# Pooled attention and a top-1 mixture of experts on one core: the first two pairs of heads are turned on TensorE instead of VectorE

## The chip, the core and the metric

The kernel runs on one core of a Trainium2 chip. The metric is the device time of one execution in microseconds (us), as the median of several runs. A difference of less than about 0.2% between two versions can't be told from none.

## What is computed

The reference, cut to what matters. Batch 8, 8 heads, 1152 positions, head dimension 64; then 4608 tokens of 512 go to one of 8 experts each.

```python
def _attn_ref(q, k, v):
    q_pool = q.reshape(B, H, S // 2, 2, D).mean(axis=3)      # two neighbouring queries become one
    scores = 1.0 / np.sqrt(D) * np.matmul(q_pool, k.transpose(0, 1, 3, 2))
    scores = scores - np.max(scores, axis=-1, keepdims=True)
    attn = np.exp(scores)
    attn = attn / (np.sum(attn, axis=-1, keepdims=True) + 1e-09)
    return np.matmul(attn, v)

def _moe_ref(x, w_gate, w1, w2):
    logits = x @ w_gate
    expert_idx = np.argmax(logits, axis=1)
    gate_w = softmax(logits)[np.arange(N), expert_idx]
    for e in range(E):
        mask = expert_idx == e
        out[mask] = gate_w[mask, None] * (np.maximum(x[mask] @ w1[e], 0.0) @ w2[e])
```

## The kernel before, in words

Attention goes by pairs of heads: 8 batches of 4 pairs, 32 pairs in all. For a pair, keys, queries and values are loaded (`load_pair`, L474), keys and queries are brought into a layout with the head dimension on the partitions (`kT`, `qT`: two heads of 64 on the 128 partitions), and then each half of the 576 pooled queries (288 columns) goes through these steps:

- **scores** (L556): 9 blocks of keys. A block is four products of 64x64 weights with 288 moving columns in the four quarters of the array (L573). VectorE copies each block from PSUM into `s`, scaled, and keeps the least value (L577, "eviction"). After the ninth block the stabilizer is reduced and spread (L598, L595, L601: `top`, `bias`).
- **exponentials**: ScalarE, two blocks at a time, in place (L605).
- **row sums** (`chunk_sum`, L635): GpSimd adds the nine blocks into three, in two additions of 128x1728 and a third of 128x576 (L661, L665, "folds"), and TensorE adds the rest (L655, L648).
- **values** (L696): 9 blocks of four products (L709) into `pa`, then `xT`.

How keys and queries are turned before: the loads put 32 numbers of a head's row beside each other on a partition, so every run in memory is 128 bytes long (`quarters`, L488). VectorE then transposes in squares of 32 (`turn_k`, L535: three instructions of 128x384 for a pair; `turn_q`, L540: two of 128x288). Before that the two neighbouring queries are added, for the first pair on VectorE (L516), for the others on GpSimd (L527). The first pair (`opening`, L484) has its keys loaded in two parts, and the queries of the first two pairs are asked for by ScalarE's queue (L501). All other loads come from SyncE (SP), in the order of its stream.

What sets the order: every step is recorded in a `Flow` (L96) with an engine, a cost in ns and a key. `emit` (L126) plays the steps through with these costs and writes each engine's instructions in the order in which they would start. The chip then runs each engine's stream in order, with semaphores between them. So costs that are given to a step shape the order, not the time. Buffers have numbers of places: three pairs of PSUM banks `st` for scores (also used by row sums and the spread), four of `s`, two of `kp`, one each of `qn` (raw queries) and `qp` (added queries). With one place for `qn`, a load of queries waits until the ones before are used up.

TensorE begins with two products of ones with 512 columns (`warm_up`, L1358), before any data is there.

After attention come the experts; their order on TensorE is the same before and after the change.

## Time and profile before

| | us |
|---|---|
| median of three runs | 1130.89 (1130.54 to 1132.59) |
| the profiled execution | 1137.59 |
| its span | 1135.8 |
| attention, until the last values | about 672 |

The profile has the busy time of each engine, a timeline of instructions in order of time, the chain of work that ended last, and busy times by stretch. In a timeline row stand the start, the duration (of a merged run of instructions: from the first start to the last end), the engine, the line and operation, the tiles, and in brackets the idle time before with what ended it. A product in 32-bit floats stands there as two records, so a block of four products is "x8". Rows on "SPq" or "ACTq" are DMA issues. A record of TensorE includes some 0.2 us after the columns have streamed, so records overlap, and a busy TensorE need not be at its peak.

### The profile page before, as it was taken

Reading aid. Unit: us, or ns where it says so; the run is one execution under the profiler, and the core shown is the slowest. Engines: PE = TensorE matmul, PEld = TensorE weight load, DVE = VectorE, ACT = ScalarE, POOL = GpSimd, SP = SyncE. Lnnn points to the kernel's source line nnn. Section 1 sums busy time; section 2 is a strip of 40 time slices with the busy share of each in tenths; the row PEclk is TensorE's granted clock in tenths of the full one; section 3 lists DMA queues with packets and bytes.
Section 4 is the critical chain, followed back from the end, with each engine's and each line's share of the span. In section 5 each row is a group of like instructions: output and inputs, shape, how many; then the busy total and the mean of one; then the engine's idle time right before and its main releaser. Section 6 shows DMA issues by size and latency. Waiting matters only on the chain.

```text
span 1135.8 us, 32903 instructions
## 1 busy us (share of the span) xinstructions
PE 1109.3 (98%) x13233; PEld 790.7 (70%) x13233; DVE 879.8 (77%) x2250; ACT 617.2 (54%) x831; POOL 851.2 (75%) x488
## 2 busy tenths in 40 slices
PE   7999999999999999999999998999999999999997
PEld 3556565565565565565655557988899989899986
DVE  6988988988988988989989849866556655567761
ACT  1666565565656556656557346444444544465551
POOL 1999999999999999999999852577566655445421
PEclk9999999999999999999999999999999999999999
DMA  9976756737747648647544417855556656667740
GB/s 133 153 135 102 150 80 115 122 51 133 120 65 129 105 71 136 99 79 137 97 80 95 134 50 219 229 173 165 168 179 200 196 171 187 197 224 261 244 157 30
DMA packets 398111, 158.07 MB, mean 139 GB/s; under 512 B 314454, under 2 KB 368626, under 8 KB 397950
## 3 DMA queue, kind: packets, MB, share of 16 engines
q1 hardware_dynamic: 378014, 133.93, 54.9%
q0 software_dynamic: 10464, 20.78, 5.9%
q10 hardware_dynamic: 9472, 1.18, 0.9%
q8 instruction: 106, 1.74, 0.7%
q14 instruction: 55, 0.45, 0.2%
HBM read 135.02 MB, written 22.07 MB: 138 GB/s over the span
## 4 chain that ended last, share of the span: by engine, by line
PE 69%; DVE 17%; issue 7%; DMA 3%; POOL 2%; ACT 1%; SPq 0%; POOLq 0%; ACTq 0%; DVEq 0%
PE pa L709 17%; PE st L573 16%; PE py L1321 16%; PE ph L1291 14%; DVE s L577 9%; DVE kT L537 2%; PE st L655 2%; DVE row L876 2%; PE st L648 1%; POOL fold L665 1%; DMA kp<-in_k_dram 1%; DMA qn<-in_q_dram 1%; DVE lw L799 1%; DVE st L812 0%; ACT w2h L1248 0%
## 5 line engine op out<-in xcount | busy, mean ns | idle before, releaser
L605 ACT ACTIVATE s<-s,bias 128x1152 f32<-128x1152 f32 (+1 forms) x320 | 351.2, 1152 | 185.2 <-DVE bias L601 183.5
L577 DVE TENSOR_SCALAR_CACHE_REDUCE s<-st 128x576 f32<-128x576 f32 x576 | 417.2, 749 | 42.9 <-PE st L573 30.6
L573 PE MATMUL st<-qT,kT 64*64 64x288 f32 x4608 | 364.0, 410 | 11.2 <-DVE s L577 4.4
L709 PE MATMUL pa<-s,vn 64*64 64x288 f32 x4608 | 351.6, 404 | 1.1 <-DVE xT L716 0.7
L573 PEld LDWEIGHTS st<-qT,kT 64*64 64x64 f32 x4608 | 167.3, 134 | 134.2 <-DVE s L577 41.6
L709 PEld LDWEIGHTS pa<-s,vn 64*64 64x64 f32 x4608 | 174.8, 133 | 106.0 <-DVE xT L716 11.4
L665 POOL TENSOR_TENSOR fold<-s 128x1728 f32<-128x1728 f32 x55 | 212.9, 3872 | 19.9 <-ACT s L605 19.2
L665 POOL TENSOR_TENSOR fold<-fold,s 128x1728 f32<-128x1728 f32 x55 | 212.8, 3869 | 0.9
L1291 PE MATMUL ph<-xh,w1h 128*128 128x248 f32 (+4 forms) x512 | 154.3, 301 | 2.3 <-DVE hl L1301 2.2
L1291 PE MATMUL ph<-xl,w1h 128*128 128x248 f32 (+4 forms) x512 | 153.3, 299 | 0.2 <-DVE xl L1165 0.2
L1291 PE MATMUL ph<-xh,w1l 128*128 128x248 f32 (+4 forms) x512 | 152.9, 299 | 0.0
L1165 DVE TENSOR_TENSOR w2l<-raw,w2h 128x1024 fp32r<-128x1024 f32 x64 | 78.1, 1222 | 80.0 <-ACT w2h L1248 72.3
L1022 POOL DMA_INDIRECT xr<-x_runs,ix x76 | 91.4, 1202 | 50.8 <-issue 24.5
L1321 PE MATMUL py<-w2h,hh 128*128 128x512 f32 x328 | 128.1, 391 | 0.0
L1321 PE MATMUL py<-w2l,hh 128*128 128x512 f32 x328 | 127.8, 390 | 0.0
L1321 PE MATMUL py<-w2h,hl 128*128 128x512 f32 x328 | 127.8, 390 | 0.0
L1330 POOL DMA_INDIRECT out_dram<-y,rec x41 | 44.4, 1082 | 86.5 <-ACT y L1338 67.2
L1299 ACT ACTIVATE hh<-ph 128x372 fp32r<-128x372 f32 (+4 forms) x100 | 49.3, 493 | 110.0 <-PE ph L1291 102.1
L1291 PEld LDWEIGHTS ph<-xh,w1h 128*128 128x128 f32 x512 | 96.1, 188 | 5.2 <-DVE hl L1301 3.9
L1291 PEld LDWEIGHTS ph<-xl,w1h 128*128 128x128 f32 x512 | 96.2, 188 | 1.2 <-DVE xl L1165 0.4
L1291 PEld LDWEIGHTS ph<-xh,w1l 128*128 128x128 f32 x512 | 96.1, 188 | 0.0
L1022 POOL DMA_INDIRECT xq<-x_runs,ix x52 | 61.5, 1182 | 45.1 <-PE py L1321 22.1
(219 smaller groups left out, 1326.1 us busy)
## 6 DMA issues: line engine op xcount, KB each, us to landing
raw<-in_moe_w_dram SPq DMA_DIRECT2D x128, 512.0 KB
kp<-in_k_dram SPq DMA_DIRECT2D x124, 144.0 KB
vn<-in_v_dram SPq DMA_DIRECT2D x124, 144.0 KB
qn<-in_q_dram SPq DMA_DIRECT2D x120, 144.0 KB
x_runs<-row SPq DMA_DIRECT2D x96, 99.0 KB
xr<-x_runs,ix POOLq DMA_INDIRECT x76
x_runs<-empty SPq DMA_DIRECT2D x4, 297.0 KB
qn<-in_q_dram ACTq DMA_DIRECT2D x16, 72.0 KB
```

The source lines that it names most:

```text
L537: nc.vector.transpose(view(kT.t.rearrange(f"p (c b i) -> p {order} i", b=NQD, i=BL)), view(kp.t.rearrange(f"p ({order}) d -> p {order} d", ...
L573: nc.tensor.matmul(pt.t[to, h, :HQ], x.kT.t[up, c * P + i * D:c * P + (i + 1) * D], x.qT.t[up, cols], start=True, stop=True, tile_position ...
L577: nc.vector.tensor_scalar(s.t[:, c], pt.t[:, :, :HQ], -SCALE, None, op0=ALU.mult, op1=ALU.min, accum_out=mx.t[:, c:c + 1],)
L605: nc.scalar.activation(s.t[:, c0:c0 + n], s.t[:, c0:c0 + n], AF.Exp, bias=bias.t, scale=-1.0)
L665: add = lambda to, a, b: nc.gpsimd.tensor_tensor(to, a, b, ALU.add)
L709: mark.made = nc.tensor.matmul(pa.t[cs, i, :HQ], x.vn.t[up, h, c, :], s.t[up, c, h], start=c == 0, stop=c == NC - 1, tile_position=(up.sta ...
L1022: ins = nc.gpsimd.indirect_dma_start(out=x.xr[i // NQD].t[:, i % NQD, :], out_offset=None, in_=xg, in_offset=bass.IndirectOffsetOnAxis(ap= ...
L1165: (nc.gpsimd if eng == "POOL" else nc.vector).tensor_tensor(lo, raw, hi.bitcast(F32), ALU.subtract)
L1291: mark.made = nc.tensor.matmul(view()[:, i, :], a[:, c, fp], b[:, c, :n], start=c == 0 and k == 0, stop=c == NDC - 1 and k == 2)
L1299: a = f.add("ACT", act(nb * n) - 44, lambda home=home, apart=apart: nc.scalar.activation(home(0), apart(), AF.Relu), at - 20, done(p), [ph ...
L1321: mark.made = nc.tensor.matmul(py.t, blocks(a)[:, c * x.nr + r], b[:, c % 2, :], start=c == 0 and k == 0, stop=c == NFC - 1 and k == 2)
L1330: ins = nc.gpsimd.indirect_dma_start(out=out, out_offset=bass.IndirectOffsetOnAxis(ap=x.re.t.bitcast(I32)[:, r, 0:1], axis=0), in_=y.t, in ...
```

## The change

For the first two pairs a new function, `first_pair`, takes the place of the loads, additions and transposes. Rows of the inputs are loaded as they lie in memory: a partition gets whole rows, 768 to 2304 bytes in a run for the keys and 4608 for the queries. TensorE multiplies them with the identity as the moving operand, which turns them: for the keys four products of 64x64 weights and 64 moving columns for a block (`cross_k`), for a half of the queries 36 products of 32 rows, 64 columns of weights and 32 moving columns (`cross_q`); the two neighbouring queries are added by accumulation in PSUM. Each result lands in a place of `st`; ScalarE copies one head's 64 partitions out, VectorE the other's. Values are loaded in one DMA for a pair. GpSimd and VectorE lose their additions and transposes for these two pairs.

```diff
-        opening = not o.exact and b == 0 and hp == 0
+        opening = not o.exact and b == 0 and hp < 2
...
+        if opening:
+            return first_pair(o, f, key, hp, x, kp, qn)
...
+    def first_pair(o, f, key, hp, x, kp, qn):
...
+        def load_k(c0, n):
+            for h, up in enumerate(both):
+                o.load(runs()[up, :, c0:c0 + n], heads(k, 0, hp)[h].rearrange("(i p c) d -> p i c d", i=2, c=NC)[:, :, c0:c0 + n])
+
+        def load_q(u, load):
+            for h in range(2):
+                load(pairs_()[h * D + u * BL:h * D + (u + 1) * BL].rearrange("p n d -> p (n d)"),
+                     heads(q, 0, hp)[h].rearrange("(i u n) d -> u i (n d)", i=BL, u=2)[u])
+
+        at = key + K_LOAD
+        cuts = [(0, NC)] if hp else [(0, FIRST), (FIRST, NC - FIRST)]
+        k0 = [f.carry("SP", 950, lambda c0=c0, n=n: load_k(c0, n), at + i, (), [kp], 100 + 300 * n, 1500 * i) for i, (c0, n) in enumerate(cuts)]
+        q0 = [f.carry("SP" if u or hp else "ACT", 950, lambda u=u: load_q(u, o.load if u or hp else side), at + 2 * u, (), [qn], 1400, 0 if hp else 2500 * u) for u in range(2)]
+        x.v = f.carry("SP", 500, lambda: o.load(vn.t.rearrange("p h c d -> p h (c d)"),
+                                                heads(v, 0, hp).rearrange("h (p c) d -> p h (c d)", p=P)), at + 3, (), [vn], 2700)
...
+        def turned(fn, ns, n, to, key, after, holds):
+            pt = score_banks(o)
+            t = f.add("PE", ns, lambda: fn(pt), key, after, [pt, *holds], QUADS)
+            copy = [(lambda up=up, h=h, eng=eng: eng(to.t[up, n], pt.t[up, h, :n.stop - n.start]))
+                    for h, (up, eng) in enumerate(zip(both, (nc.scalar.copy, nc.vector.tensor_copy)))]
+            made = done(*(f.add(e, w(n.stop - n.start), c, key, done(t), [pt, to]) for e, w, c in zip(("ACT", "DVE"), (act, dve), copy)))
...
+        def cross_k(c0, n, pt):
+            for c in range(n):
+                for i in range(2):
+                    for h, up in enumerate(both):
+                        at = (2 * c + i) * D
+                        nc.tensor.matmul(pt.t[up, h, at:at + D], runs()[up, i, c0 + c], ident[up, up], start=True, stop=True,
+                                         tile_position=(up.start, up.start))
+
+        def cross_q(u, pt):
+            for m in range(HQ // BL):
+                for t in range(2):
+                    for h, to in enumerate(both):
+                        up = slice(to.start + u * BL, to.start + (u + 1) * BL)
+                        nc.tensor.matmul(pt.t[to, h, m * BL:(m + 1) * BL], pairs_()[up, 2 * m + t], ident[up, up], start=t == 0, stop=t == 1,
+                                         tile_position=(up.start, to.start))
+
+        def turn_k(c0, n, at, got):
+            made = turned(lambda pt: cross_k(c0, n, pt), 220 * n, slice(c0 * P, (c0 + n) * P), kT, key + at, done(got), [kp])
...
+        def turn_q(u, at, got):
+            x.q[u] = turned(lambda pt: cross_q(u, pt), 1000, slice(u * HQ, (u + 1) * HQ), qT, key + at, done(got), [qn])
+
+        turn_k(0, FIRST, 0, k0[0])
+        turn_q(0, 1, q0[0])
+        for c0 in range(FIRST, NC, TURN):
+            turn_k(c0, min(TURN, NC - c0), 2 + c0 / 2, k0[-1])
+        turn_q(1, 7, q0[1])
```

Where instructions stand now. Lines after the change are 43 higher for scores, values and folds (L573 is L616, L709 is L752, L665 is L708); L574 are the products that turn keys, L582 those that turn queries.

TensorE at the start of the program, before; `st` are places in PSUM, and 16 blocks of scores follow each other:

```order
L1360 MATMUL st_210<-ones 128x512 x2
L573 MATMUL st_251<-qT_242,kT_249 64x288 x4
L573 MATMUL st_256<-qT_242,kT_249 64x288 x4
L573 MATMUL st_264<-qT_242,kT_249 64x288 x4
L573 MATMUL st_282<-qT_242,kT_249 64x288 x4
```

and after:

```order
L1403 MATMUL st_210<-ones 128x512 x2
L574 MATMUL st_230<-ident,kp_216 64x64 x12
L582 MATMUL st_243<-ident,qn_213 64x32 x36
L616 MATMUL st_286<-qT_283,kT_280 64x288 x4
L574 MATMUL st_291<-ident,kp_216 64x64 x12
L574 MATMUL st_307<-ident,kp_216 64x64 x12
L616 MATMUL st_322<-qT_283,kT_280 64x288 x4
L616 MATMUL st_329<-qT_283,kT_280 64x288 x4
L582 MATMUL st_335<-ident,qn_213 64x32 x36
L616 MATMUL st_373<-qT_283,kT_280 64x288 x4
```

Five turns (three of keys, two of queries) now stand in TensorE's stream, among the first three blocks of scores.

TensorE from the spread of the first stabilizer on, before (`pa` are the first values):

```order
L595 MATMUL st_375<-ident,top 64x64 x4
L573 MATMUL st_384<-qT_242,kT_249 64x288 x4
L573 MATMUL st_392<-qT_242,kT_249 64x288 x4
L709 MATMUL pa_403<-s_261,vn_231 64x288 x4
L573 MATMUL st_409<-qT_397,kT_389 64x288 x4
L709 MATMUL pa_403<-s_261,vn_231 64x288 x8
```

and after:

```order
L638 MATMUL st_448<-ident,top 64x64 x4
L616 MATMUL st_455<-qT_283,kT_280 64x288 x4
L574 MATMUL st_462<-ident,kp_225 64x64 x12
L582 MATMUL st_476<-ident,qn_380 64x32 x36
L616 MATMUL st_517<-qT_283,kT_280 64x288 x4
L616 MATMUL st_524<-qT_283,kT_280 64x288 x4
L752 MATMUL pa_530<-s_304,vn_223 64x288 x8
L574 MATMUL st_542<-ident,kp_225 64x64 x12
L574 MATMUL st_555<-ident,kp_225 64x64 x12
L616 MATMUL st_572<-qT_283,kT_280 64x288 x4
L752 MATMUL pa_530<-s_304,vn_223 64x288 x8
L582 MATMUL st_589<-ident,qn_380 64x32 x36
```

The spread stands after 13 blocks instead of 16, and all five turns of the second pair stand between the first values.

SyncE's loads, before (`kp` keys, `vn` values, `qn` queries; each `x4` with 32x36 is one pair):

```order
L485 DMA kp_218<-in_k_dram 32x12x32 x4
L485 DMA kp_218<-in_k_dram 32x24x32 x4
L485 DMA vn_231<-in_v_dram 32x9x64 x8
L485 DMA kp_244<-in_k_dram 32x36x32 x4
L485 DMA vn_298<-in_v_dram 32x2x576 x4
L485 DMA kp_314<-in_k_dram 32x36x32 x4
L485 DMA qn_414<-in_q_dram 32x36x32 x4
L485 DMA vn_443<-in_v_dram 32x2x576 x4
L485 DMA kp_474<-in_k_dram 32x36x32 x4
L485 DMA qn_572<-in_q_dram 32x36x32 x4
```

and after:

```order
L485 DMA kp_216<-in_k_dram 64x2x192 x2
L485 DMA kp_216<-in_k_dram 64x2x384 x2
L485 DMA qn_213<-in_q_dram 32x1152 x2
L485 DMA vn_223<-in_v_dram 128x2x576
L485 DMA kp_225<-in_k_dram 64x2x576 x2
L485 DMA vn_228<-in_v_dram 128x2x576
L485 DMA qn_380<-in_q_dram 32x1152 x4
L485 DMA kp_403<-in_k_dram 32x36x32 x4
L485 DMA qn_634<-in_q_dram 32x36x32 x4
L485 DMA vn_665<-in_v_dram 32x2x576 x4
L485 DMA kp_700<-in_k_dram 32x36x32 x4
L485 DMA qn_748<-in_q_dram 32x36x32 x4
```

14 issues for the first two pairs instead of 24 (and on ScalarE's queue 2 instead of 16). The queries of the third pair, `qn_414` before and `qn_634` after, have to wait for the place of the second pair's: before, until GpSimd had added them, now, until TensorE has done the last of the products on `qn_380`.

GpSimd's own stream, in words (a fold here is one addition of 128x1728): before, it held two folds, the addition of queries for the third pair, a third addition (128x576), two folds, a fold of the next pair, a third addition, a fold, the addition of queries for the fourth pair and a third addition. Now it holds two folds, a third addition, the addition of queries for the third pair, two folds, the addition of queries for the fourth pair, a third addition, two folds, an addition of queries and a third addition.

## Rows read from the trace of the kernel before

**Rows 1.** Busy time by stretch: start:end, us, then each engine with its instructions

```profile
core 0: us, PE busy (x) PEld busy (x) DVE busy (x) ACT busy (x) POOL busy (x), PEclk, DMA share, GB/s
28.00:100.00 72.00, 71.39 (x1171) 42.47 (x1160) 64.21 (x187) 47.60 (x51) 70.47 (x26) 1.00 0.74 130
```

**Rows 2.** Timeline of GpSimd, from the first fold on

```profile
28.23 3.87 POOL L665 TENSOR_TENSOR fold<-s 128x1728 f32<-128x1728 f32 x1 [6.04 <-ACT s L605]
...
37.21 1.41 POOL L527 TENSOR_TENSOR qp<-qn 128x576 f32<-128x576 f32 x1 [1.14 <-DMA qn<-in_q_dram]
...
39.93 3.88 POOL L665 TENSOR_TENSOR fold<-s 128x1728 f32<-128x1728 f32 x1
...
47.73 3.88 POOL L665 TENSOR_TENSOR fold<-s 128x1728 f32<-128x1728 f32 x1
...
59.52 7.71 POOL L665 TENSOR_TENSOR fold<-s 128x1728 f32<-128x1728 f32 x2
...
175.81 1.40 POOL L527 TENSOR_TENSOR qp<-qn 128x576 f32<-128x576 f32 x1 [2.56 <-DVE top L598]
```

**Rows 3.** Timeline of the opening: warm-up, first addition of queries, first scores, first exponentials

```profile
1.27 3.78 PE L1360 MATMUL st<-ones 128*128 128x512 f32 x4 [1.27 <-DVE ones L323]
...
7.47 0.46 DVE L516 TENSOR_TENSOR qp<-qn 128x288 f32<-128x288 f32 x1 [2.87 <-DMA qn<-in_q_dram]
...
8.96 3.16 PE L573 MATMUL st<-qT,kT 64*64 64x288 f32 x24 [3.90 <-DVE kT L537]
...
24.61 5.36 ACT L605 ACTIVATE s<-s,bias 128x1152 f32<-128x1152 f32 x5 [22.15 <-DVE bias L601]
```

**Rows 4.** The chain that ended last, first load of keys: start, us, what

```profile
1.41 2.97 DMA kp<-in_k_dram
```

**Rows 5.** Timeline of TensorE: the spread among other blocks, and a row-sum group

```profile
30.75 0.29 PE L595 MATMUL st<-ident,top 64*64 64x64 f32 x8
30.86 0.67 PE L709 MATMUL pa<-s,vn 64*64 64x288 f32 x8
31.35 1.68 PE L573 MATMUL st<-qT,kT 64*64 64x288 f32 x24
...
53.88 1.18 PE L655 MATMUL st<-fold,ones 128*32 128x288 f32 x16
54.99 0.71 PE L573 MATMUL st<-qT,kT 64*64 64x288 f32 x8
```

**Rows 6.** Timeline of TensorE: three products of 96 weight columns and 16 moving ones

```profile
111.95 0.68 PE L731 MATMUL st<-sums_of,sm 128*96 128x16 f32 x6
```

**Rows 7.** Groups by line and shape, ScalarE and VectorE: count, busy us, mean ns

```profile
L605 ACT ACTIVATE s<-s,bias 128x1152 f32<-128x1152 f32 x256 | 305.6, 1247 | 185.2 <-DVE bias L601 183.5 <-POOL fold L665 1.3
...
L715 ACT COPY xT<-pa 128x288 f32<-128x288 f32 x64 | 24.7, 386 | 72.8 <-PE pa L709 61.5 <-PE st L573 10.6
...
L537 DVE STREAM_TRANSPOSE kT<-kp 128x384 f32<-128x384 f32 x96 | 53.1, 567 | 0.8 <-DMA kp<-in_k_dram 0.8
...
L541 DVE STREAM_TRANSPOSE qT<-qp 128x288 f32<-128x288 f32 x64 | 29.1, 464 | 0.1
```

**Rows 8.** Timeline of VectorE: two evictions that follow each other, and a stabilizer

```profile
18.79 0.75 DVE L577 TENSOR_SCALAR_CACHE_REDUCE s<-st 128x576 f32<-128x576 f32 x1
...
19.47 0.75 DVE L577 TENSOR_SCALAR_CACHE_REDUCE s<-st 128x576 f32<-128x576 f32 x1
...
24.28 0.29 DVE L601 TENSOR_REDUCE bias<-st 128x1 f32<-128x128 f32 x1
```

**Rows 9.** Products of scores (first row) and of values (second) until 32.3 us

```profile
0.00:32.30 32.30, 16.97 (x184) 7.15 (x188) 1.00 0.96 134
...
0.00:32.30 32.30, 4.13 (x48) 1.98 (x48) 1.00 0.96 134
```

**Rows 10.** Timeline of SyncE's issues: loads of the third and fourth pair

```profile
29.36 5.09 SPq L485 DMA_DIRECT2D qn<-in_q_dram  x4
34.50 2.07 SPq L485 DMA_DIRECT2D vn<-in_v_dram  x4
36.67 4.88 SPq L485 DMA_DIRECT2D kp<-in_k_dram  x4
```

More of the change, by code (lines that the diff above doesn't have):

```diff
@@ L530, in load_pair @@
-        q1 = [q1[0], q1[-1]]
-        o.asked = q0[-1] and q0[-1][9][0]
-        key += K_PIECE + (START if start and not opening else 0)
+        if opening:
+            return first_pair(o, f, key, hp, x, kp, qn)
+        k0 = k_part(0, rows, 1900, 2600, done(o.asked))
+        q0 = f.carry("SP", 1900, lambda: quarters(qn.t.rearrange("p j b t d -> p (j b t) d"), heads(q, b, hp)), key + K_LOAD, (), [qn], 2600)
+        vb = heads(v, b, hp).rearrange("h (p b c) d -> b p h (c d)", b=NQD, c=NC)
@@ L543, in turned @@
         def turned(half):
[L544 removed]
+            x.q[half] = done(f.add("DVE", turn_ns(HQ), lambda: turn_q(half), key + 7 * half, done(q1), [qT, qp]))
             o.turned.extend(x.q[half])
```

57 lines of the change are left out of this document (22 added, 35 removed).

## Prediction

> **What bounds the kernel now.** I read the busy times by stretch first. Between 28 and 100 us GpSimd is busy for 70.47 of 72 us, TensorE for 71.39, VectorE for 64.21 [rows 1]. TensorE's figure is blown up, since its records overlap; so I asked the timeline which of the two waits. GpSimd has no idle time in front of the folds at 39.93, 47.73 and 59.52 [rows 2]. The exponentials that the fold at 47.73 needs are three of the five records that start about 41.1 us, so they were there near 44.8: ScalarE, and TensorE behind it, run some 2.9 us ahead. **GpSimd's additions set the pace** after the opening, and the opening sets when they begin: the first fold starts at 28.23, after 6.04 us without work that exponentials ended [rows 2]. Much later there is a wait of 2.56 us for VectorE [rows 2], so the two sides are close, and a gain on GpSimd alone can't run far.
>
> In the opening [rows 3], warm-up products start at 1.27 and end about 4.85 without their tail. Queries are on the chip at 7.47, scores start at 8.96 and take 3.16 us for three blocks (24 records), where 24 records later take 1.68 [rows 5]: half the clock; exponentials start at 24.61.
>
> **What is taken away.** From VectorE two additions of 0.46 [rows 3], and for each of two pairs two turns of 0.464 and three of 0.567 [rows 7]. It works on evictions meanwhile, 0.68 us apart [rows 8]. From GpSimd the additions of the second pair, 1.58 us (two halves, about the 1.41 of a whole one plus 0.17 for a second start) [rows 2]. This is the only work taken from the engine that paces.
>
> **What is added.** TensorE turns three blocks of keys with two products after each other in each quarter, 12 times the 0.056 us between records (the spread's eight records take 0.11 of start times before the next product at 30.86, two per product and four quarters at once [rows 5]): 0.67 us. Half the queries are 36 products, two at a time, each in two records: 36 record times. No row has 64 weight columns with 32 moving ones. Below, the moving columns decide: half of 0.056, 1.0 us. Above, the weights decide: six records of 96 weight columns and 16 moving ones take 0.68 in all, less 0.24 of tail 0.09 each [rows 6], far above what 16 columns take, so a record with 64 weight columns keeps 0.056: 2.0 us. I take the upper end, since this row is nearest in its few moving columns. A change of the tile's shape costs 0.14 (16 records from 53.88 to the next product at 54.99, 1.11 in place of 0.97 [rows 5]), some 0.25 for both ways: **2.25 us a turn of queries**. At half the clock all is doubled.
>
> The Trainium skill ("TensorE: Matmul & The Clock Gate", section "LDWEIGHTS (loading the stationary operand)") says that loading weights scales with their columns and not with rows; the rows 6 just read agree, and by that rule halving the moving columns saves nothing.
>
> Each turn then needs copies of 288 or 384 columns on ScalarE and VectorE, 0.39 to 0.45 [rows 7]. A copy and the semaphores beside it put about 0.65 between a turn and the first score.
>
> **The start.** The first keys are on the chip at 4.4 now [rows 4]; longer runs won't be later. Queries are needed when the first turn of keys ends, at 6.2; with 2 issues in place of 16 I take them as there, and if they still come at 7.47 all of the start is 1.3 later. So warm-up gates. Scores begin at 4.85 + 1.34 (keys at 1.2 GHz, which is what the first blocks' doubled spacing shows [rows 3]) + 2.25 + 0.65 = 9.1, against 8.96: nothing gained. Then in TensorE's order come a block (0.49), two turns of keys (1.34), two blocks (0.97) and a turn of queries (2.25): the fourth block ends 5.1 after the start, where VectorE's evictions take over. Nine of them at 0.68 and 0.45 for stabilizer and spread [rows 8] bring the first exponentials 12.4 after the start, to 21.5, **3.1 us earlier** than 24.61: before, VectorE also turned things there. The first fold follows 5.6 later, after four and a half exponentials of 1.25 [rows 7], near 27.1 instead of 28.23: **1.1 us earlier**.
>
> **The price on TensorE.** In all, two pairs cost 2 x (3 x 0.67 + 2 x 2.25) = 13 us. The last turn of the second pair ends about 23.1 after the first score, at 32.2, with 21 blocks done. Before, 184 records of scores and 48 of values are there by 32.3 [rows 9], 29.5 blocks with half-done ones. TensorE is thus 8.5 blocks, 4.2 us, late. GpSimd now takes the second pair's first folds after the first pair's last ones and after two additions of queries, some 7 us later in its stream; with the 2.9 us lead this covers 4.2.
>
> **What is late next: the queries of the third pair.** Their place is free when that last turn ends, 32.2. From the first issue to use it takes 7.85 (issue at 29.36, used at 37.21 [rows 10, 2]); at the shortest the 5.09 of issuing and an estimated microsecond to land, 6.1. They arrive at 40.05, or at 38.3. GpSimd has done two folds and a third by 27.1 + 2 x 3.87 + 1.41 = 36.3 and waits. After the addition it stands at 41.5 (39.7), where before the same work was done at 39.93. SyncE meanwhile issues queries (5.1), values (2.1), keys (4.9) [rows 10] and only then the next queries, at 44.3 (43.2) once the place is free: use at 52.1 (49.3), while GpSimd's two folds are done at 49.2 (47.4). A second wait of 2 to 3 us. Addition, third fold and the next two folds and addition take 10.55 more: 64.05 (61.25). Before, the same work is done at 59.52 plus the 1.4 of the addition that stood later: 60.9. So GpSimd ends between 0.3 and 3.1 us late. What it was spared, 1.58 + 1.1, is spent in waits for loads that a slower TensorE releases.
>
> I take the middle, 1.7. Nothing idle follows until 145 us or so, so it stays. The profiled execution, 1137.59 us with a span of 1135.8, is 6.7 us above the median; I put the difference on the median: 1130.89 + 1.7 = **1132.6 us**, its own range 1130.9 (the 2.56 us wait at 175.81 swallows it) to 1134.0. A measurement of this kernel can tell about 0.2%, 2.3 us, so this counts as no change.
>
> **Rivals.**
> - *The query turns run at the pace of their moving columns.* Each is 1 us shorter; four of them bring the place of the queries free 4 us earlier, less the spacing that VectorE sets; GpSimd then ends at 60.1 or 57.3 instead of 60.9: 0.8 to 3.6 us faster, middle 1128.7. For it: nobody waits for weights in the blocks of scores. Against it: the rows of 96 columns.
> - *TensorE's lag is not covered* (the other side). If the 2.9 us lead is smaller in the second pair, because its scores now stand behind all turns, folds wait for exponentials, and all 4.2 us arrive at the end: 1135.1, slower. It decides from where the lag exceeds the lead plus what GpSimd was pushed back. For it: TensorE's 71.39 of 72 and the wait of 2.56 for VectorE; against: no wait of GpSimd from 37.2 to 100 us but for loads.
> - *The clock stays at 1.2 GHz through the turns.* The first scores then start at 11.1, and the next turns take 3.3 us more; first exponentials at 26.8, later than before; the whole 5.3 on top of the forecast is 1137.9, half the turns still warm some 1136, which I take. For it: before, even a row of 24 full products went at half pace after the warm-up. Against: that came after idle time of 3.90, which is gone.
> - *Nothing comes of it*: the earlier loads end behind warm-up, the pace of evictions gives the first exponentials no earlier, GpSimd's spared work becomes idle: 1130.9.
>
> On the third the Trainium skill has a rule ("TensorE: Matmul & The Clock Gate", "Part 4: PE-mode transpose"): the full clock does not engage for transposes on TensorE. These are plain products with an identity, so it bears on them only by likeness, and no run here shows it yet.
>
> **How the numbers follow.** Forecast 0.40, of it faster 0.03, same 0.30, slower 0.07. Column pace 0.24: faster 0.18, same 0.06, since its span straddles the bound. Lag 0.18 and clock 0.12: slower. Nothing 0.06: same. Together faster 0.21, same 0.42, slower 0.37. The range takes in the early end of the column pace, 1127.3, and the middle of the clock, 1136.2.
>
> **What would show it.** In the changed profile: first scores near 9.1; records of a query turn 56 ns apart (28 for the first rival); first exponentials near 21.5 and first fold near 27.1; two waits of GpSimd for queries between 36 and 53 us; some 21 blocks done at 32 us. Exponentials behind which folds wait after 54 us would show the second rival; first scores beyond 10 the third. The forecast fails if GpSimd meets no wait for loads, or if the folds after 60 us stand more than 2 us from where they stood.

## The result, and the profile after

The changed kernel takes 1138.55 us (median of six runs, 1137.14 to 1142.09) against 1131.93 for the kernel before in the same comparison: a ratio of 1.0061, 95% interval 1.0048 to 1.0075. By this ratio it is **slower by 6.9 us** (the medians differ by 6.6), where 1.7 us and a time of 1132.6 were forecast and the range ended at 1136.2. Two later comparisons of the unaltered kernels gave 1.0046 and 1.0054, some 5 to 6 us.

One remark on reading the runs: they come from several sessions on several chips, in which the median of the kernel before lies between 1131 and 1139 us (one chip showed 1131.46 in one session and 1138.24 in another). Every ratio is taken against runs of the kernel before on the same chip in the same session, and profiles are laid side by side only for the first 100 us or from one session.

The opening of TensorE in the profile of the changed kernel (timeline: start, duration, engine, line and operation, tiles, count, in brackets the wait before):

```profile
5.64 1.54 PE L574 MATMUL st<-ident,kp 64*64 64x64 f32 x22 [0.18 <-DMA kp<-in_k_dram]
7.11 4.05 PE L582 MATMUL st<-ident,qn 32*64 32x32 f32 x72
12.14 1.24 PE L616 MATMUL st<-qT,kT 64*64 64x288 f32 x8 [0.99 <-ACT qT L563]
13.16 2.66 PE L574 MATMUL st<-ident,kp 64*64 64x64 f32 x45
17.65 2.29 PE L582 MATMUL st<-ident,qn 32*64 32x32 f32 x72
19.86 6.39 PE L616 MATMUL st<-qT,kT 64*64 64x288 f32 x80
```

The same 72 records of a query turn (L582) take 4.05 us at 7.11 and 2.29 us at 17.65: the first at the lower clock level (1.2 GHz), the second at the full one (2.4 GHz). A step, from one product's record to the next on the same quarter of the array, is 0.107 us in the first and 0.058 in the second. The granted clock doesn't show this here: the trace of this execution has no record of it before 17.4 us, and where there is none the view prints 1.00. First scores start at 12.14, against 8.96 [rows 3].

A second profile of the changed kernel was taken together with one of the kernel before on the same chip (below, "three kernels on one chip"). TensorE there:

```profile
6.59 2.29 PE L582 MATMUL st<-ident,qn 32*64 32x32 f32 x72
9.86 1.24 PE L616 MATMUL st<-qT,kT 64*64 64x288 f32 x8 [0.99 <-ACT qT L563]
10.88 2.35 PE L574 MATMUL st<-ident,kp 64*64 64x64 f32 x45
...
14.51 1.70 PE L582 MATMUL st<-ident,qn 32*64 32x32 f32 x50 [0.24 <-ACT kT L563]
16.62 0.88 PE L582 MATMUL st<-ident,qn 32*64 32x32 f32 x22 [0.41 <-issue]
17.43 6.39 PE L616 MATMUL st<-qT,kT 64*64 64x288 f32 x80
```

Here the first query turn had the full clock, and the first scores started at 9.86. So the opening differs by 2.3 us between executions of one kernel, and the first profile is the worse case. In both, the block of scores and the turns of keys behind it run at the lower level (a block of eight records in 1.24 against 0.71 later; two turns of keys in 2.35 and 2.66 instead of 1.34). In this second profile the granted clock shows it (busy times by stretch; the column before the last two is the clock), and so it does in a third one of the changed kernel (below, "a further profile"; second row):

```profile
9.35:12.70 3.35, 2.84 (x43) 2.37 (x45) 0.80 (x3) 0.68 (x2) 0.00 (x0) 0.50 1.07 209
```

```profile
8.30:15.00 6.70, 5.72 (x82) 4.46 (x78) 2.79 (x6) 1.34 (x3) 0.00 (x0) 0.50 0.88 224
```

It is 1.00 ahead of these stretches, from 5.9 and 4.8 us on, and behind them. GpSimd in the second profile, and in the kernel before on the same chip:

```profile
30.33 3.85 POOL L708 TENSOR_TENSOR fold<-s 128x1728 f32<-128x1728 f32 x1 [26.08 <-DVE s L620]
...
42.51 1.41 POOL L506 TENSOR_TENSOR qp<-qn 128x576 f32<-128x576 f32 x1 [2.90 <-DMA qn<-in_q_dram]
...
54.62 1.41 POOL L506 TENSOR_TENSOR qp<-qn 128x576 f32<-128x576 f32 x1 [2.92 <-DVE s L620]
...
66.50 1.42 POOL L708 TENSOR_TENSOR fold<-fold 128x576 f32<-128x576 f32 x1
67.87 7.71 POOL L708 TENSOR_TENSOR fold<-s 128x1728 f32<-128x1728 f32 x2
```

```profile
28.12 3.87 POOL L665 TENSOR_TENSOR fold<-s 128x1728 f32<-128x1728 f32 x1 [6.33 <-DVE kT L537]
...
37.51 1.41 POOL L527 TENSOR_TENSOR qp<-qn 128x576 f32<-128x576 f32 x1 [1.56 <-DVE xT L716]
...
59.82 7.71 POOL L665 TENSOR_TENSOR fold<-s 128x1728 f32<-128x1728 f32 x2
```

The first fold starts 2.2 us later instead of 1.1 earlier, and GpSimd then meets the two waits that were forecast, 2.90 and 2.92 us. (The second is put down to VectorE, whose work there had long been done; SyncE's stream below shows the load, and the first profile puts the wait of 2.87 us at the same place down to it.) The seventh fold starts at 67.87 instead of 59.82; 1.4 of these 8.05 us are one more addition of queries done by then, so GpSimd is **6.6 us late**. The busy times of the two in the stretch of [rows 1], the changed kernel first:

```profile
28.00:100.00 72.00, 68.62 (x1186) 40.95 (x1186) 60.82 (x174) 44.67 (x50) 63.53 (x23) 1.00 0.74 126
```

```profile
28.00:100.00 72.00, 71.27 (x1168) 42.55 (x1160) 64.07 (x187) 47.50 (x51) 70.17 (x26) 1.00 0.79 128
```

GpSimd, the engine that sets the pace, is busy for 63.53 us instead of 70.17: the missing 6.6 us are the same loss, seen as idle time.

### The profile page after: what moved, and what is told of

Same layout as the page of the kernel before. It is cut to its first block, busy times and chain, and to the rows that moved or that the text cites. A ratio compares the mean times of both kernels' runs of the same rounds, so it can differ in the third digit from the quotient of the medians.

```text
span 1140.5 us, 33739 instructions
## 1 busy us (share of the span) xinstructions
PE 1123.0 (98%) x13665; PEld 805.5 (71%) x13665; DVE 879.5 (77%) x2248; ACT 621.7 (55%) x841; POOL 852.5 (75%) x486
## 4 chain that ended last, share of the span: by engine, by line
PE 69%; DVE 17%; issue 6%; DMA 3%; POOL 3%; SPq 1%; ACT 1%; POOLq 0%; DVEq 0%; ACTq 0%
PE py L1364 17%; PE pa L752 16%; PE ph L1334 15%; PE st L616 15%; DVE s L620 10%; DVE kT L514 2%; PE st L698 2%; DVE row L919 2%; DMA vn<-in_v_dram 2%; SPq L485 1%; PE st L691 1%; POOL fold L708 1%; PE st L582 1%; PE st L574 1%; DVE lw L842 1%
## 5 line engine op out<-in xcount | busy, mean ns | idle before, releaser
L616 PE MATMUL st<-qT,kT 64*64 64x288 f32 x4608 | 361.6, 408 | 5.3 <-DVE s L620 3.2
L752 PE MATMUL pa<-s,vn 64*64 64x288 f32 x4608 | 351.9, 406 | 0.9 <-DVE xT L759 0.7
L616 PEld LDWEIGHTS st<-qT,kT 64*64 64x64 f32 x4608 | 166.1, 133 | 122.8 <-DVE s L620 39.7
L752 PEld LDWEIGHTS pa<-s,vn 64*64 64x64 f32 x4608 | 173.8, 133 | 106.7 <-issue 11.8
L708 POOL TENSOR_TENSOR fold<-s 128x1728 f32<-128x1728 f32 x55 | 212.9, 3873 | 35.2 <-DVE s L620 28.5
L708 POOL TENSOR_TENSOR fold<-fold,s 128x1728 f32<-128x1728 f32 x55 | 212.9, 3873 | 0.9
```

Of the source, the lines that this page charges most:

```text
L616: nc.tensor.matmul(pt.t[to, h, :HQ], x.kT.t[up, c * P + i * D:c * P + (i + 1) * D], x.qT.t[up, cols], start=True, stop=True, tile_position ...
L708: add = lambda to, a, b: nc.gpsimd.tensor_tensor(to, a, b, ALU.add)
L752: mark.made = nc.tensor.matmul(pa.t[cs, i, :HQ], x.vn.t[up, h, c, :], s.t[up, c, h], start=c == 0, stop=c == NC - 1, tile_position=(up.sta ...
```

## The experiments

**Three kernels on one chip: does the loss at 60 us reach the end?** Before, changed, and the keys-only kernel (below), unaltered.

> The kernel before, unaltered, for a profile from the same chip as the changed kernel's and the keys-only kernel's beside it, since before and changed kernel had their profiles from different chips so far. Theory: first fold at 28 to 28.5, GpSimd busy 70 to 71 of the 72 us from 28 to 100; ratio 1.000 within its interval. Rival (the opening of this kernel varies): a first fold off by over 1 us.

> The changed kernel, unaltered, on the same chip as before_third. Theory (what GpSimd loses until 60 us reaches the end): GpSimd's work after the addition for the fifth pair's queries 5 to 8 us behind before_third's, and the time 5 to 7 us over it; the loss until the first fold 2 to 4.5 us, depending on the clock in the first turn of queries, the rest in two waits for queries. Rival (what is lost in the opening is caught up later, and the loss comes elsewhere): the difference in GpSimd's stream shrinks to under 3 us by 300 us.

Measured: 0.9999 (0.9989 to 1.0008) and 1.0054 (1.0041 to 1.0067). Against the profile of the kernel before, the folds of the changed kernel stand 2.2 us later at the first, 8.0 at 60 us, 8.2 at 230, 8.5 at 490 and 9.4 at the last fold of attention. Nothing is caught up in attention: the rival falls, and most of the loss arises before 60 us. Less the 1.4 of the addition it is 6.6 us at 60. From 230 us on both kernels have done the same additions, so the 8.2 to 9.4 there are all loss: 2 to 3 us come later. In the time it is 6.1 us (0.0054 of 1138.75), and the two profiled executions are 7.2 apart, so part of it is made up behind attention; where, no run here shows.

**A further profile of the changed kernel and of the kernel before.**

> The changed kernel itself once more, unaltered: the four profiles of the first job showed the clock rising at times that differ from execution to execution (17.65 us in the profile of the changed kernel, 12.6 us in another kernel with the same opening), and the profiled execution of the changed kernel was the longest of its six. Theory (the clock's rise differs by execution, and one profile shows one case): the first query turn at least partly at 0.058 us a step instead of 0.107, first exponentials 2 to 3 us earlier than 27.14, waits of GpSimd for two loads of queries still there, the median again 5 to 8 us over the kernel before. Rival (the profile was typical, the turns always run at half the clock): first exponentials within 0.5 us of 27.14.

Measured 1.0046 (1.0032 to 1.0059). First scores at 9.74, first exponentials at 24.73, first fold at 30.35, waits of 2.48 and 3.30 us: the theory. The first query turn fell from steps of 0.058 to 0.107 us in its last products, at 8.2 us, where the granted clock falls to 0.50; TensorE had worked without a pause since 5.4 us.

> The kernel before itself, unaltered, for a second profile of its opening: a run that kept its opening but for later lines showed the first fold at 32.49 us, where the profile shown has 28.23. Theory (the clock's rise differs by execution and moves the first fold by some us, in this kernel too, so that one profile's first fold is no measure): first products at 0.480 us a block until some moment between 12 and 20 us, the first fold anywhere from 27 to 33, ratio 1.000 within its interval. Rival (the kernel before has a steady opening): first fold within 0.7 us of 28.23.

Measured 0.9997 (0.9982 to 1.0011), and the theory was wrong here: the first fold stood at 28.09. The kernel before has a steady opening. Scores start after an idle time of 3.2 to 3.9 us at the lower level in every profile (0.480 us for four records, half a block; 0.24 at the full level) and the clock rises between 17 and 18 us; its three profiles have the first fold within 0.15 us. The spread is the changed kernel's, whose turns begin right behind the warm-up, where the clock is up in some executions and not in others.

**The first pair alone.**

```diff
-        opening = not o.exact and b == 0 and hp < 2
+        opening = not o.exact and b == 0 and hp < 1
```

> Only the first pair is loaded in natural runs and turned on TensorE; the second pair is loaded, added on GpSimd and turned on VectorE like any later pair. Theory (the opening turns run at half the clock and hold the first fold back to 32.76 us; the second pair costs GpSimd two waits for queries of 3.27 and 2.87 us): first fold near 31 to 33 us, no wait of GpSimd for queries of 2 us or more after 40 us, and about half of the loss left: 2 to 4 us over the kernel before. Rival (the second pair's turns, squeezed between the first values, make TensorE late, and the opening costs nothing at the end): within 1 us of the kernel before.

Measured 1.0021 (1.0010 to 1.0031), 2.4 us. As the theory had it, but for the first fold (30.21, just ahead of the range) and for a wait of 2.47 us for the third pair's queries at 36.55, which came ahead of 40.

**The second pair alone** (on the kernel before):

```diff
+        if not o.exact and b == 0 and hp == 1:
+            return first_pair(o, f, key, hp, x, kp, qn)
```

> The first pair as before (VectorE turns), only the second pair in natural runs and on TensorE. Theory: first fold at 28 to 29 us as before, query turns of the second pair 2.3 us each at the full clock, waits of GpSimd for the third and fourth pair's queries of 2 to 4 us each; 2 to 4 us over the kernel before. Rival (all of the loss is the opening at half clock): within 1 us of the kernel before.

Measured 1.0027 (1.0017 to 1.0037), 3.1 us: 2.4 and 3.1 add up to 5.5, about the whole loss. That needn't mean that each pair loses its share in the same way in the changed kernel, for the path was another than expected. The opening is the old one, there was one wait for queries of 0.49 us, and yet the first fold stood at 32.49. ScalarE's timeline shows why:

```profile
26.30 2.40 ACT L674 ACTIVATE s<-s,bias 128x1152 f32<-128x1152 f32 x2 [1.63 <-DVE bias L670]
30.49 0.39 ACT L589 COPY qT<-st 64x288 f32<-64x288 f32 x1 [1.79 <-DVE qT L589]
30.78 0.47 ACT L589 COPY kT<-st 64x384 f32<-64x384 f32 x1
31.15 1.26 ACT L674 ACTIVATE s<-s,bias 128x1152 f32<-128x1152 f32 x1
```

The third exponential of the first pair could go at 28.7, when the second ends, but in ScalarE's stream a copy of the second pair's turned queries stands ahead of it, and that waits for TensorE's turn (27.66 to 29.95) and for VectorE's copy. **A copy on ScalarE is a new wait in front of the exponentials.** In the changed kernel the same copies spread the three exponentials that the first fold needs over 5.6 us instead of 3.6; the prediction had that sum for another reason (four and a half exponentials), so by luck. No run here moves these copies alone to another engine's stream, so how much of the 3.1 us is theirs isn't shown.

**Two places for raw queries**, on the changed kernel and, as parts and control, on three others:

```diff
-        qn = tile_of(o, "qn", [P, NJ, NB, 2, BL], pool=o.ld)
+        qn = tile_of(o, "qn", [P, NJ, NB, 2, BL], bufs=2, pool=o.ld)
...
-        f = Flow(dict(st=S_BUFS, s=UNITS, qn=1,
+        f = Flow(dict(st=S_BUFS, s=UNITS, qn=2,
```

> The changed kernel with two places for raw queries, so that a load need not wait until TensorE has read the pair before. Theory: GpSimd's waits of 3.27 and 2.87 us go or shrink below 1 us, the first fold stays near 32.8 us, and the time falls by 2 to 5 us against the changed kernel, to 2 to 4 over the kernel before. Rival (the waits only fill time that GpSimd would have spent waiting for exponentials): waits of the same length ended by ScalarE, and less than 1 us gained.

> Only the first pair on TensorE, with two places for raw queries. With one place this was 2.4 us over the kernel before, with a wait of GpSimd of 2.47 us for the third pair's queries at 36.55 us. Theory (the wait for a place makes most of that loss): no such wait, first fold near 30, 0 to 1.2 us over the kernel before. Rival (the late first exponentials make it): 2 us or more over the kernel before all the same.

> Only the second pair on TensorE, with two places for raw queries; with one place this was 3.1 us over the kernel before. Theory (the place is half of the loss, the rest is TensorE's 6.5 us of turns among the second pair's scores and first values): 1 to 2.5 us over the kernel before. Rival (the place is all of it): within 0.8 us of the kernel before. Rival (the turns are all of it): 2.6 us or more over it.

> The kernel before with two places for raw queries, as a control: what does the second place bring by itself? Theory (the wait for the place is a cost of the changed kernel, since TensorE holds it until its last query turn; before, GpSimd frees it as soon as it has added): within 1.2 us of the kernel before. Rival (a second place is a gain in any version, and the runs with it say nothing on the change): 2 us or more faster than the kernel before.

Measured, one place and two:

| on TensorE | one place | two places |
|---|---|---|
| neither (before) | 1 | 0.9990 (0.9974 to 1.0005) |
| first pair | 1.0021 | 1.0006 (0.9995 to 1.0017) |
| second pair | 1.0027 | 1.0026 (1.0013 to 1.0038) |
| both (the change) | 1.0061, 1.0046, 1.0054 | 1.0029 (1.0019 to 1.0039) |

The waits for queries go, as GpSimd's timeline of the changed kernel with two places shows: the additions at 33.38 and 45.21 start without waiting, and what waits now is a fold, for exponentials.

```profile
33.38 1.41 POOL L506 TENSOR_TENSOR qp<-qn 128x576 f32<-128x576 f32 x1
...
41.38 3.88 POOL L708 TENSOR_TENSOR fold<-s 128x1728 f32<-128x1728 f32 x1 [1.28 <-ACT s L648]
45.21 1.40 POOL L506 TENSOR_TENSOR qp<-qn 128x576 f32<-128x576 f32 x1
```

So the second place takes away about half of the loss of the change (2 to 3.6 us by the three comparisons; against 1.0046 the intervals overlap). The first fold, forecast near 32.8, came at 29.58, since this profile's first query turn had the full clock. What the place does is seen in SyncE's stream: with one place the second pair's queries are asked for at 17.53, when the first pair's second turn is done, and the third pair's at 35.37; with two, at 7.23 and 21.13. By the table it lies with the first pair (1.7 us, though those two intervals touch, and no gain for the second).

The edit changes the planned order too, so the runs don't part the place from the order: in the changed kernel the addition of queries now stands right behind the first fold, and with the first pair alone it stands ahead of it and still waits for its load until 31.86, so that the first fold came at 33.23, not near 30 as expected. For the second pair alone the place is nothing; that leaves the turns with their copies, as the second rival had it. The control gained too little to tell (its interval includes none). And the state at 60 us tells the end only to some 2 us: with two places the changed kernel is 1.2 to 1.6 us late there by the same count (against the two later profiles of the kernel before), and 3.3 us in the time.

**One copy instead of two.** Both heads' results in one PSUM bank, and ScalarE copies 128 partitions.

```diff
-            copy = [(lambda up=up, h=h, eng=eng: eng(to.t[up, n], pt.t[up, h, :n.stop - n.start]))
-                    for h, (up, eng) in enumerate(zip(both, (nc.scalar.copy, nc.vector.tensor_copy)))]
+            made = done(f.add("ACT", act(n.stop - n.start), lambda: nc.scalar.copy(to.t[:, n], pt.t[:, 0, :n.stop - n.start]), key, done(t), [pt, to]))
```

In the changed kernel the two copies of a turn do not run side by side. VectorE's and ScalarE's rows of the first query turn:

```profile
11.20 0.46 DVE L563 COPY qT<-st 64x288 f32<-64x288 f32 x1 [3.43 <-PE st L582]
```

```profile
11.70 0.39 ACT L563 COPY qT<-st 64x288 f32<-64x288 f32 x1 [3.42 <-DVE qT L563]
```

ScalarE starts when VectorE is done; 1.0 us pass from turn to scores, where the prediction had 0.65.

> The changed kernel with both heads' results in one PSUM bank, copied out by one instruction on ScalarE instead of one on ScalarE and one on VectorE that wait for each other. Theory (the two copies of a turn run one after the other, about 1.1 us a turn, and VectorE's share of them holds up evictions): from the end of the first query turn to the first score about 0.6 us instead of 1.2, evictions without copies between them, first fold 0.5 to 2 us earlier than in the changed kernel with the same clock; the time falls by 1 to 3 us against the changed kernel. Rival (the copies hide beside TensorE): under 0.7 us gained.

Measured 1.0056 (1.0042 to 1.0070) beside 1.0046 for the changed kernel on the same chip. From the end of the turn to the first score it was 0.50 us as expected, and the first fold 0.8 us earlier than in the profile with the same clock (31.97 against 32.76), but nothing of it can be seen in the time, where 1 to 3 us were expected. With both edits:

> Both: two places for raw queries, and one copy on ScalarE. Theory: the gains add, 3.5 us (two places, measured) and 1 to 3 us: 0 to 2.5 us over the kernel before. Rival (with the waits for loads gone, GpSimd waits for exponentials and the second gain is lost or the first): no better than the two places alone, 3 us over the kernel before.

Measured 1.0012 (1.0000 to 1.0024), against 1.0029 with the places alone. Whether the single copy adds anything stays open: the intervals overlap, and the two were on different chips.

**Fewer products in the turns of queries.**

```diff
-                for t in range(2):
+                for t in range(1):
```

> The changed kernel with 18 products instead of 36 in each turn of queries: the even queries alone are turned, the sum of two neighbours is left out. Theory (the turns of queries stand on the path to the first fold and to the place of the queries): a turn takes 2.0 us in the opening instead of 4.05, 1.15 later instead of 2.29; first scores near 10.1, first exponentials near 24, the last turn of the second pair ends 4 to 5 us earlier, and the time falls by 3 to 6 us against the changed kernel. Rival (TensorE has room, the copies and VectorE's evictions set the pace): under 1.5 us gained.

Its time (ratio 1.1029) can't be used: with other queries other tokens go to other experts, and the experts' part is longer. Attention can be read. The turns took 1.24 us (the clock was up in both), first scores came at 8.56, first exponentials at 21.71, the first fold at 26.86, and at 98 us GpSimd stood 5.0 us ahead of the further profile. The turns of queries do stand on the path. Half the products took half the time, at 0.058 us a step as before; and a step of the keys' turns, with 64 moving columns instead of 32 and the same 64 columns of weights, is 0.058 too (24 records in 0.88 us, of which 0.2 is the tail). So the moving columns don't set the pace of these products. That the loading of weights does fits this, but no run changes the weights.

**The clock.** A product of ones in the pause before the first scores, and a longer warm-up:

```diff
+        if hp == 0:
+            f.add("PE", 300, lambda: nc.tensor.matmul(o.pw.t[:, 0], ones, ones.unsqueeze(1).broadcast_to([P, 4, P]), start=True, stop=True),
+                  key + 1, done(o.last), [o.pw])
```

> The changed kernel with one more product of ones, 512 columns, between the first turn of queries and the first scores, where TensorE waits 1.2 us for the copies; its result goes unused. Theory (TensorE's pause there lets the clock fall, and keys' turns and first scores run at 0.107 us a step): after the extra product the steps stay at 0.058, the fourth block of scores ends 1.5 to 3 us sooner after the first, and the time falls by 1 to 2.5 us against the changed kernel. Rival (the clock falls after products that use a part of the array, pause or not): steps of 0.107 after it all the same, and a change under 1 us, or up to 1 us longer.

```diff
-WARM = 2
+WARM = 4
```

> The changed kernel with four products of ones before the data instead of two; nothing else differs. It starts TensorE's first turn later, by 1.7 us where the clock is up after the first two, 3.4 where it isn't. Theory (the clock falls in the turn of queries whatever stood before, and what stands ahead of the first scores arrives late in full at the first fold): first scores 1.5 to 3.5 us later than 9.7 to 12.1, steps of 0.107 us in the turns of keys again, first fold 1 to 3.5 us later, and 1 to 3 us more than the changed kernel. Rival (a longer warm-up keeps the clock up through the opening): steps of 0.058 in all turns, the fourth block of scores no later than before, and no loss or a gain.

The filled pause gave 1.0056 (1.0042 to 1.0070), no gain: the granted clock had already fallen inside the turn, at 8.2 us, and the product of ones itself took 2.08 us. There, and in the further profile, the pause wasn't the cause. In the profile from one chip, and in that with two places, the clock fell inside the pause (at 9.3 and 9.2 us), and for these the run decides nothing. The longer warm-up, TensorE:

```profile
8.61 2.29 PE L582 MATMUL st<-ident,qn 32*64 32x32 f32 x72
10.83 1.61 PE L574 MATMUL st<-ident,kp 64*64 64x64 f32 x48
12.37 2.28 PE L582 MATMUL st<-ident,qn 32*64 32x32 f32 x70
16.40 0.30 PE L582 MATMUL st<-ident,qn 32*64 32x32 f32 x2 [1.74 <-issue]
16.62 5.71 PE L616 MATMUL st<-qT,kT 64*64 64x288 f32 x60
```

All turns ran at the full level, as its rival said, and still it was the slowest version: 1.0091 (1.0075 to 1.0108). The order of TensorE's stream had changed with the warm-up's planned cost: all turns now stand ahead of the first scores, which start at 16.62, after a pause of 1.74 us. And the granted clock, 1.00 from 7.1 to 17.3 us, is 0.50 from 17.3 to 20.7, under the first scores. A higher clock in the turns was bought with a later start, so this run doesn't show what the clock alone would have given.

The Trainium skill ("TensorE: Matmul & The Clock Gate", "Part 4: PE-mode transpose") says that the full clock does not engage for TensorE's transpose mode. These are plain products with an identity; here they ran from 7.8 to 14.7 us at a granted clock of 1.00, so they don't always pull it down. In the further profile and in that with the filled pause it fell inside such a turn, at 8.2 us, after some 3 us of them, as the rule would have it for a transpose; whether the kind of product was the reason isn't shown.

**Keys alone on TensorE.** On the kernel before: keys of the first pair in natural runs, turned on TensorE with one copy on ScalarE; values in one load; queries as before.

```diff
-            k0 = [k_part(0, cut, 1200, 1200), None]
+            k0 = [f.carry("SP", 950, lambda: load_k(0, FIRST), key + K_LOAD, (), [kp], 1000), None]
...
+            if opening:
+                pt = score_banks(o)
+                t = f.add("PE", 220 * n, lambda c0=c0, n=n, pt=pt: cross_k(c0, n, pt), key + 2 + c0 / 2, done(k0[c0 >= FIRST]), [pt, kp], QUADS)
+                e = f.add("ACT", act(n * P), lambda c0=c0, n=n, pt=pt: nc.scalar.copy(kT.t[:, c0 * P:(c0 + n) * P], pt.t[:, 0, :n * P]), key + 2 + c0 / 2, done(t), [pt, kT])
```

> The kernel before with only the keys and values of the first pair loaded in natural runs and its keys turned on TensorE, one copy on ScalarE for a turn; queries of both pairs and the keys of the second as before. Theory (turns of queries, 2.3 us or 4.05 at half the clock, the copies before the first score, and the place of the raw queries make the loss; turns of keys fit into TensorE's idle time before 9 and around 12 to 14 us and spare VectorE three turns of 0.567): first scores at 8 to 9 us as before, first exponentials 2 to 5 us before 24.61, GpSimd's fold at 28.23 not later than before and its waits for loads under 1.5 us; 0.5 to 3 us faster than the kernel before. Rival (any turn on TensorE in the opening, where the clock is at half, costs more than VectorE's): equal to or over the kernel before.

> The keys-only kernel, unaltered, on the same chip as before_third. It was 0.18% faster although its first fold stood at 30.39 us. Theory (the fold after it meet no wait for queries, and what the late start costs is less than what is saved): GpSimd less than 1 us behind before_third from 60 us on, or ahead of it, and a ratio of 0.997 to 0.999. Rival (its gain was chance): a ratio of 0.9995 or more.

Measured 0.9982 (0.9972 to 0.9992) and, on another chip, 0.9979 (0.9970 to 0.9988): **faster than both kernels**, by some 2 us than the one before. But the opening was later, not earlier: first scores at 13.10, first fold at 30.39. VectorE's wait and SyncE's issues:

```profile
11.98 0.46 DVE L530 TENSOR_TENSOR qp<-qn 128x288 f32<-128x288 f32 x1 [7.38 <-DMA qn<-in_q_dram]
```

```profile
4.39 6.96 SPq L485 DMA_DIRECT2D kp<-in_k_dram  x4
```

SyncE, done early with the first pair, loads the second pair's keys from 4.39 on, and the queries, half of them still to be issued by ScalarE, land at 11.98 instead of 7.47. GpSimd still stands level with the kernel before at 53 us (0.1 us ahead until 290 us, same chip), since its folds meet no wait for queries, where before waited 1.56; at the last fold of attention it is 1.1 us behind. Where the 2 us lie isn't seen in the profiles, which have equal spans; that stays open. With queries asked for first:

```diff
-            q0[1] = q_part(mid, rows, 1600, 1700)
+            q0[1] = q_part(mid, rows, 1600, 1700, False)
```

where the last argument lets SyncE ask for them (the second pair's queries go by SyncE too).

> The kernel with the first pair's keys alone on TensorE, but the second half of its queries, and the second pair's queries, asked for by SyncE ahead of the second pair's keys instead of by ScalarE. There the first scores started at 13.10 us, since queries landed at 11.98 behind the second pair's keys, and it was 1.7 us faster all the same. Theory (the opening counts at the end): first scores at 7.5 to 10 us, first fold 2 us or more before 30.39, and 1 us or more faster than with the late queries. Rival (GpSimd's work after the first fold decides, the opening is made up for at the batch's end): earlier scores, and a time within 0.8 us of that kernel's ratio of 0.9982.

Measured 0.9967 (0.9954 to 0.9980), **3.8 us faster than before**, the lowest ratio of all. That it is faster than the kernel before is shown; its lead over the run with the late queries (0.9982 and 0.9979) is not, since the intervals overlap. First scores came at 10.38 only, but the first fold 3.6 us earlier than with the late queries, and GpSimd is 2.5 us ahead of the kernel before on the same chip at 40 and at 60 us (37.37 against 39.88, 56.95 against 59.44):

```profile
26.82 3.88 POOL L684 TENSOR_TENSOR fold<-s 128x1728 f32<-128x1728 f32 x1 [3.00 <-DVE s L596]
...
37.37 3.85 POOL L684 TENSOR_TENSOR fold<-s 128x1728 f32<-128x1728 f32 x1
...
56.95 7.72 POOL L684 TENSOR_TENSOR fold<-s 128x1728 f32<-128x1728 f32 x2
```

## Why the prediction was wrong

**Right:** the engine that bounds (GpSimd; its lag at 60 us, 6.6, is near the loss in the time), 2.25 us for a query turn at the full clock (2.22 from its first product to the next block's, steps of 0.058: the rival with the moving columns falls), that the scores start no earlier for the earlier loads, and the two waits for queries: 2 to 3 us each forecast, 2.90 and 2.92 measured, 3.27 and 2.87 in the first profile. The 5.6 us from first exponentials to first fold came out by luck, as said above. The rival that TensorE's lag isn't covered didn't happen: at both places GpSimd waited for loads, the first of which SyncE issued when the last query turn was done (at 35.4, forecast 32.2). With these waits gone (two places) a fold does wait 1.28 us for exponentials, so that lag stands close behind. SyncE's issues in the profile from one chip:

```profile
35.37 3.54 SPq L485 DMA_DIRECT2D qn<-in_q_dram  x4
...
46.60 3.67 SPq L485 DMA_DIRECT2D qn<-in_q_dram  x4
```

**Wrong, the clock (first step that failed).** "Then in TensorE's order come a block (0.49), two turns of keys (1.34), two blocks (0.97)" took the full clock from the first query turn on. The rows ahead of the prediction showed the lower level until the third block [rows 3], and I let that hold for the first turn of keys only. In the profile from one chip, first scores to first exponentials took 14.85 us (9.86 to 24.71), not 12.4: **2.5 us**, all of it ahead of the fourth block, which starts 7.57 us after the first scores instead of the 5.1 of the sum. Some 1.4 of it is the lower level, under the first block and the two turns of keys (granted clock 0.50 from 9.3 to 12.7); the rest is a wait for a copy of keys ahead of the second query turn and a pause of 0.41 inside it, for which the sum had nothing. In the other two profiles the lower level lasts until 17.4 and 15.0 us, no such pause is there, and the fourth block starts 7.7 us after the first scores: there it is the clock alone, 2.7 us. In the first profile the first query turn ran low too, another 1.8. The rival on the clock had the right place; its whole price, 1137.9, was nearer than the middle that I gave it (partly by luck, since it stood on the miscount below), and its chance of 0.12 was too low for something the trace had shown.

**Wrong, the start.** First scores came at 9.86, not 9.1. Most records of the first turn of keys waited for their load until 5.63, where I took 4.4 from [rows 4] and let the warm-up gate at 4.85, though that row was for another shape of load: 0.8, of which the turn gave 0.4 back, since it ran at the full level. And the copies run one after the other, 0.4 more than the 0.65 put down. Together **0.8 us**.

**Wrong, the count of GpSimd's work.** "Before, the same work is done at 59.52 plus the 1.4 of the addition that stood later" forgot that one addition of 128x576 (also 1.4) was missing on the other side. The two cancel; the comparison is with 59.52, and my own numbers give a lag of 1.7 to 4.5 us, in the middle **3.1, not 1.7**. By the bound that I named myself this would have been a forecast of slower.

**Wrong, what GpSimd was spared.** "This is the only work taken from the engine that paces" put 1.58 us on the additions of the second pair. In the trace of the kernel before they stand ahead of the first fold (28.23), between idle times of GpSimd:

```profile
19.75 0.79 POOL L527 TENSOR_TENSOR qp<-qn 128x288 f32<-128x288 f32 x1 [15.50 <-DMA qn<-in_q_dram]
21.40 0.79 POOL L527 TENSOR_TENSOR qp<-qn 128x288 f32<-128x288 f32 x1 [0.86 <-DMA qn<-in_q_dram]
```

So the change took nothing from GpSimd while it paced. The sum didn't use the 1.58, but the sentence that says what was spared and spent did.

Smaller slips in the working: the 5.1 us at which "the fourth block ends" is where it starts, and 12.4 is 0.7 us more than the terms beside it add up to, about what that block takes; 184 and 48 records are 29 blocks, not 29.5; and "10.55 more" leaves out the addition itself, which the 64.05 has. The estimated microsecond from the last issue of queries to their landing came from no row: from the end of the issues to the use 2.8 us passed before the change, and 3.6 and 4.4 after it.

Together: 1.7 + 1.4 + 2.5 + 0.8 = 6.4 us; GpSimd's lag measured 6.6, and the time 5.2 to 6.9.

## What to carry to other kernels

Work that is moved off the pacing engine pays only if nothing that the engine waits for is put behind the moved work: here the place of a raw input was held by the slower new user, and copies stood ahead of exponentials in a stream that runs in order. Look first whether the work that is taken away stood where that engine paced or where it idled. Price work of TensorE in an opening at the clock that the opening's own rows show. When two streams are compared at a point, count every kind of instruction done on each side; one forgotten addition was the step from no change to slower.

## What was not expected of the hardware

The same turn in the same kernel ran at 0.107 us a step in one execution and at 0.058 in another, from the same start, which shifts its opening by 2.3 us. The granted clock shows the lower level only where the trace has records of it: 0.50 in two profiles of the changed kernel, and a printed 1.00 before 17.4 us in the one that ran low throughout, so there the spacing of records has to be read. TensorE paused for 1.74 us with nothing to wait for in the profile inside a long run of short products (near 14.7 us in the run with four warm-up products; 1.67 in the one with two places and one copy, 0.41 in the changed kernel). And queries landed at 11.98 instead of 7.47 us when SyncE loaded the keys and values of the first pair in long runs and went on with the second pair's keys: ScalarE, which asks for these queries, stood still after three issues until 5.34 us instead of 3.19. Which of these loads held them back isn't shown.
